# First batch element of a delta-rule and MLP-mixer kernel: block layout by vector transposes, zero products on TensorE, a new order of loads and steps

## The chip, the cores and the metric

The kernel runs on one core of one Trainium2 chip. Its engines are TensorE (PE; its weight loads are shown as PEld), VectorE (DVE), ScalarE (ACT), GpSimd (POOL) and SyncE (SP, which here issues nearly all DMAs). The metric is the device time of one execution in microseconds. The kernel before takes 851.35 us (median of three runs).

## The reference

Four batch elements, 8 heads of 48 numbers, 768 steps of time. For each head a 48x48 state is carried through time (the delta rule); its reads, with heads side by side (768x384), go through an MLP mixer: first over time (768 to 256 to 768), then over channels (384 to 1536 to 384).

```python
k_n = k / (np.linalg.norm(k, axis=-1, keepdims=True) + 1e-06)
for t in range(S):
    y[:, :, t] = np.einsum('bhd,bhde->bhe', q[:, :, t], state)
    v_old = np.einsum('bhde,bhd->bhe', state, kt)
    state = state + bt[:, :, :, None] * np.einsum('bhd,bhe->bhde', kt, vt - v_old)
...
h = np.maximum(xt @ w_tok1, 0.0) @ w_tok2          # xt: x with time last
u = x + h.transpose(0, 2, 1)
out = u + np.maximum(u @ w_ch1, 0.0) @ w_ch2
```

## The kernel before

**Units and steps.** The time of a batch element is cut into 6 units of 128 steps (`u` counts them through: 0 to 5 are the first element's), a unit into two chunks of 64. Inside a chunk the recurrence is solved in closed form: a triangular 64x64 matrix per head has to be inverted. Between chunks the state is carried.

**What is done for a unit.** `load_kq` loads keys and queries (`kpad`, `qpad`, and the keys a second time as `kst`). `prep` computes norms, turns keys and queries (`p_t`, L308 and L325), writes the turned keys to the block-diagonal `kbd` (one buffer), multiplies (`p_g`, L338) and masks the products into `gm` (DVE, L340). The triangular blocks' 32x32 diagonal parts are then inverted for several units at once, a *round* (`invert`): 30 steps of two DVE instructions each (L373, L377), with one block per partition. To get the blocks there, four DMAs per unit write them from `gm` to DRAM (L356) and one DMA reads them with a block in each partition (L367); afterwards one DMA writes the inverses (L384), and `fetch_w` reads them into `wt`, four DMAs per unit (L395). `join` makes the 64x64 inverses from the 32x32 ones (DVE transposes `t`, L407; products `p_z`, `p_x`).

**The recurrence.** `recur` is one chunk: `p_q` (PE), `r_bd` (DVE), `p_w` (PE), `w_bd` (ACT), `p_s` (PE), the new state `s_bd` (DVE, L486). The next chunk's `p_q` needs that state. In the first batch element each part is cut into two halves of the heads. The first element has 12 such chunks, called steps 0 to 11 here.

**The mixer.** `mixer(b)` needs all 12 chunks of element b: `p_1` (L510), `p_h` (L523), whose sum into `xb` is a DVE addition (L527), then for 6 groups of 128 time steps a turn `p_ut`, `p_c` (L549) and `p_o` (L564). While the mixer of one element runs, the units of the next are computed between its matmuls.

**Weights.** `round_weights` rounds the float64 weights to float32 in pieces: a load into `d` (L177), two ACT and two DVE instructions, an addition on POOL (L193), one more DVE instruction (L195). There are 6 pieces of 256 columns for `w1`, 4 of 384 for `w2`, 12 for `wc1` and 12 for `wc2`.

**Order.** Every function is a generator; `at(time, dt, fn, ...)` sets a time of its own scale (one unit of the first element is 1) for its first part and the distance of the next ones, and `run_plan` issues the parts in order of these times. Each engine executes its instructions in an order fixed when the program is built. Rounds are units [0, 1], [2, 3, 4, 5], then four each.

Of the kernel before, what the change touches and what calls it, by code (L numbers as in the profile page):

```python
# [23 lines left out]
def kernel(  # L24
# [70 lines left out]

    ident = const.tile([128, 128], FP32, name="ident")
# [9 lines left out]

    nc.scalar.sqrt(const.tile([1, 1], FP32, name="warm"), ident[0:1, 0:1])

# [4 lines left out]
    NW = 3  # L113
    NK = 3
# [22 lines left out]
    for t in gms:  # L137
        pad = t[:, 0 : NB * GW].rearrange("s (b three n) -> s b three n", b=NB, n=DP)
        nc.vector.memset(pad[:, :, 1, D:DP], 0.0)
        nc.gpsimd.memset(t[:, NB * GW :], 0.0)  # L140
    for t in t11s + wts + [zst]:
        nc.gpsimd.memset(t, 0.0)
# [9 lines left out]

    def load_beta():

        rows = mlp_pool.tile([B * H, S], FP32, name="b_rows", tag="xb")
        nc.scalar.dma_start(out=rows, in_=beta.rearrange("b h s -> (b h) s"))
# [8 lines left out]
        nc.scalar.copy(beta_st.rearrange("s b p c -> s c (b p)"), p_b)  # L165
        yield

    def round_weights(dst, src):
# [23 lines left out]
        )  # L192
        nc.gpsimd.tensor_tensor(out=f, in0=f, in1=lo, op=ALU.add)  # L193
# [25 lines left out]
    xins = {}  # L219
    xouts = {}  # L220
    rounds = [[0, 1], [2, 3, 4, 5]]
# [4 lines left out]
    turning = set()  # L226
    walked = set()
# [8 lines left out]
    def load_kq(u):  # L236
        b, c = divmod(u, NCH)
        ksts[u] = kst = loads.tile([128, NP, 2, D], FP32, name="kst")
# [16 lines left out]
    def load_v(u):  # L255
        vsts[u] = v_st = loads.tile([128, NP, 2, D], FP32, name="v_st")
        stacked(v_st, v, u)
        yield
        nc.gpsimd.tensor_tensor(
            out=v_st, in0=v_st,  # L260
            in1=nrms[u % NV][:, :, :, None].to_broadcast([128, NP, 2, D]), op=ALU.mult,
        )

# [6 lines left out]
    def gm_of(u):  # L270
        return gms[u % NV][:, 0 : NB * GW].rearrange(
            "s (b three n) -> s b three n", three=3, n=DP
        )

    def wt_of(u):
        return wts[u % NW][:, 0 : NB * C].rearrange("s (b n) -> s b n", n=C)

    def prep(u):
# [12 lines left out]
        )  # L291
        nrm_f = nrm.rearrange("s p c -> s (p c)")
# [3 lines left out]
        rec = work.tile([128, NB], FP32, name="rec")  # L296
        nc.vector.reciprocal(rec, nrm_f)
# [19 lines left out]
        nc.gpsimd.tensor_tensor(  # L317
# [5 lines left out]
        p_t = ps_prep([128, NP, 2, C], "p_t")  # L323
# [3 lines left out]
        nc.gpsimd.tensor_tensor(  # L327
# [3 lines left out]
        if u + NK < NU:  # L331
            load_kq(u + NK)
# [19 lines left out]
        for par in range(2):  # L352
            for i in range(2):
                lo = (4 * j + 2 * par + i) * NB
                row = C * par + HB * i
# [309 lines left out]
```

## Time and profile before

| | us |
|---|---|
| runs, median (lowest to highest) | 851.35 (850.71 to 854.84) |
| profiled execution | 852.24 |
| its span, first to last instruction | 850.4 |
| PE busy | 732.3 |
| DVE busy | 394.8 |
| ACT busy | 253.0 |
| POOL busy | 111.6 |

The span is 1.84 us shorter than the execution that it was taken from. Busy shares over the span mean little here: the first 202 us, in which the first batch element's units are computed, and the rest, in which mixers fill PE, have different limits. Mean granted TensorE clock over the span is 0.924 of full speed. "Released by" or an arrow `<-` in a row names what ended the idle time before an instruction.

### The profile page before, as it was taken

What the parts mean: (1) busy time and instruction counts of PE and PEld (TensorE: products, weight loads), DVE (VectorE), ACT (ScalarE), POOL (GpSimd) and SP (SyncE); (2) the same over time, 40 slices, a digit from 0 to 9 for tenths busy, and PEclk for the clock granted to TensorE, in tenths of its full rate; (3) what the DMA queues carried; (4) which work ended last, traced back from release to release, by engine and by line L of the source; (5) the groups of instructions that cost most, each with busy time, mean ns of one, the idle gap of its engine ahead of it and who ended that gap; (6) DMA issues with size and microseconds to landing.
All of it is one profiled execution on the core that took longest, in us unless ns stands there. A gap on an engine that the chain in (4) does not pass through costs nothing.

```text
span 850.4 us, 13384 instructions
## 1 busy us (share of the span) xinstructions
PE 732.3 (86%) x5080; PEld 606.6 (71%) x5080; DVE 394.8 (46%) x1081; ACT 253.0 (30%) x596; POOL 111.6 (13%) x142
## 2 busy tenths in 40 slices
PE   5630654969689999999999899999999999999998
PEld 4620644856469797887787888886898888678876
DVE  4487775756973459333267323493229422010000
ACT  5430422744234522333231333311332222111110
POOL 4322112223430211002000001110000000000000
PEclk9765755987899999999999999999999999999999
DMA  7763414445433441224122223202110200000000
GB/s 137 138 144 63 107 28 126 71 82 155 121 109 53 71 94 24 68 44 78 29 48 54 43 49 69 46 19 53 22 39 20 44 11 10 9 1 20 11 9 19
DMA packets 164591, 49.73 MB, mean 58 GB/s; under 512 B 155536, under 2 KB 158608, under 8 KB 164528
## 3 DMA queue, kind: packets, MB, share of 16 engines
q1 hardware_dynamic: 164480, 48.79, 26.6%
q8 instruction: 40, 0.66, 0.3%
q14 instruction: 23, 0.19, 0.1%
q10 hardware_dynamic: 48, 0.10, 0.0%
HBM read 37.85 MB, written 11.01 MB: 57 GB/s over the span
## 4 chain that ended last, share of the span: by engine, by line
PE 49%; DVE 9%; DMA 2%; ACT 2%; issue 1%; SPq 1%; ACTq 0%
PE p_c L549 16%; PE p_o L564 15%; DVE x L377 3%; DVE sub L373 3%; PE p_h L523 3%; PE p_s L482 2%; PE p_g L338 2%; PE p_q L453 2%; PE p L510 2%; PE p_w L470 2%; PE p_x L422 1%; PE p_z L413 1%; SPq L251 1%; PE p_ut L533 1%; DMA kst<-in_k_dram 1%
## 5 line engine op out<-in xcount | busy, mean ns | idle before, releaser
L549 PE MATMUL p_c<-u_t,wc 128*128 128x128 f32 x1728 | 218.2, 280 | 2.5 <-ACT u_t L537 1.8
L549 PEld LDWEIGHTS p_c<-u_t,wc 128*128 128x128 f32 x1728 | 206.5, 195 | 7.8 <-ACT u_t L537 2.5
L564 PE MATMUL p_o<-wc,r 128*128 128x384 f32 x576 | 197.5, 490 | 3.1 <-DVE wc L195 3.1
L564 PEld LDWEIGHTS p_o<-wc,r 128*128 128x128 f32 x576 | 105.0, 191 | 64.8 <-DVE wc L195 4.4
L556 ACT ACTIVATE r<-p_c 128x512 f32<-128x512 f32 x72 | 43.0, 597 | 156.8 <-PE p_c L549 156.4
L373 DVE TENSOR_TENSOR sub<-x 128x84 f32<-128x84 f32 (+22 forms) x210 | 77.3, 368 | 22.9 <-DMA x<-n_dram 18.3
L377 DVE TENSOR_TENSOR x<-x,sub 128x84 f32<-128x84 f32 (+22 forms) x210 | 76.7, 365 | 4.7
L338 PE MATMUL p_g<-kqt,kbd 128*128 128x128 f32 x384 | 60.1, 313 | 17.9 <-ACT kqt L326 17.7
L413 PE MATMUL p_z<-t,gm 128*65 128x64 f32 x384 | 30.7, 236 | 50.2 <-DVE t L407 49.8
L338 PEld LDWEIGHTS p_g<-kqt,kbd 128*128 128x128 f32 x384 | 55.1, 223 | 24.0 <-ACT kqt L326 22.5
L570 DVE TENSOR_TENSOR xb<-xb,p_o 128x384 f32<-128x384 f32 x24 | 13.3, 554 | 116.2 <-PE p_o L564 116.0
L413 PEld LDWEIGHTS p_z<-t,gm 128*65 128x65 f32 x384 | 28.7, 151 | 52.7 <-issue 28.5
L486 DVE TENSOR_TENSOR s_bd<-s_bd,p_s 64x192 f32<-64x192 f32 (+1 forms) x100 | 31.6, 316 | 73.9 <-PE p_s L482 72.2
L482 PE MATMUL p_s<-w_bd,gm 128*128 128x96 f32 x384 | 58.5, 297 | 5.2 <-ACT w_bd L474 4.9
L482 PEld LDWEIGHTS p_s<-w_bd,gm 128*128 128x128 f32 x384 | 52.6, 208 | 10.3 <-ACT w_bd L474 9.1
L340 DVE TENSOR_TENSOR gm<-p_g,mb 128x512 f32<-128x512 f32 x48 | 33.0, 690 | 57.3 <-PE p_g L338 55.0
L453 PE MATMUL p_q<-s_bd,kqt 128*128 128x96 f32 x352 | 50.9, 287 | 4.2 <-DVE s_bd L486 3.9
L453 PEld LDWEIGHTS p_q<-s_bd,kqt 128*128 128x128 f32 x352 | 47.1, 201 | 9.6 <-issue 3.0
L470 PE MATMUL p_w<-r_bd,wt 128*65 128x96 f32 x384 | 45.5, 263 | 7.2 <-issue 3.5
L455 DVE TENSOR_TENSOR r_bd<-v_st,p_q 64x192 f32<-64x192 f32 (+1 forms) x110 | 34.8, 316 | 35.1 <-PE p_q L453 23.0
L459 ACT ACTIVATE xb<-p_q 64x384 f32<-64x384 f32 (+1 forms) x55 | 23.0, 419 | 92.7 <-DVE r_bd L455 92.4
L474 ACT COPY w_bd<-p_w 64x192 f32<-64x192 f32 (+1 forms) x120 | 33.5, 280 | 54.0 <-PE p_w L470 52.0
(70 smaller groups left out, 708.8 us busy)
## 6 DMA issues: line engine op xcount, KB each, us to landing
d<-in_moe_w_ch_dram SPq DMA_DIRECT2D x24, 384.0 KB, 3.3
kpad<-in_k_dram SPq DMA_DIRECT2D x24, 192.0 KB, 3.5
kst<-in_k_dram SPq DMA_DIRECT2D x96, 48.0 KB, 2.6
qpad<-in_q_dram SPq DMA_DIRECT2D x24, 192.0 KB, 3.6
v_st<-in_v_dram SPq DMA_DIRECT2D x96, 48.0 KB, 2.6
out_dram<-xb SPq DMA_DIRECT2D x24, 192.0 KB, 1.9
n_dram<-gm SPq DMA_DIRECT2D x96, 32.0 KB, 1.7
wt<-w_dram SPq DMA_DIRECT2D x96, 32.0 KB, 2.1
```

The lines of the kernel that those rows point to most:

```text
L338: nc.tensor.matmul(p_g[:, i], kbd[:, nb], kqt[:, nb])
L373: nc.vector.tensor_tensor(out=tmp, in0=x[:, 0:s, s : s + 1].to_broadcast([n, s, w]), in1=x[:, s : s + 1, s + 1 : HB].to_broadcast([n, s, w ...
L377: nc.vector.tensor_tensor(out=x[:, 0:s, s + 1 : HB], in0=x[:, 0:s, s + 1 : HB], in1=tmp, op=ALU.add,)
L413: nc.tensor.matmul(p_z[0:65, nb], gm[:, lo : lo + 65], t11[:, nb])
L453: nc.tensor.matmul(p_q[:, p], kqt[:, 2 * p + cc], s0[:, p])
L455: nc.vector.tensor_tensor(out=r_bd[r, hp, e], in0=v_st[r, hp, cc], in1=p_q[hi, hp, e], op=ALU.subtract,)
L470: nc.tensor.matmul(p_w[0 : C + 1, p], wts[u % NW][:, w_lo : w_lo + C + 1], r_bd[:, p])
L474: nc.scalar.copy(w_bd[r, hp, e], p_w[lo, hp, e])
L482: nc.tensor.matmul(p_s[:, p], gm[:, 2 * p + cc, 0:2], w_bd[:, p])
L549: nc.tensor.matmul(p_c[:, i], wc1[:, cb, f * 128 : (f + 1) * 128], u_t[:, cb], start=(cb == 0), stop=(cb == NCB - 1),)
L556: nc.scalar.activation(r, p_c, ACTF.Relu)
L564: nc.tensor.matmul(p_o, r2[f // FG][:, f % FG], wc2[:, f], start=(f == 0), stop=(f == NHT - 1),)
```

## The change

In rounds of the first batch element (units 0 to 5) the blocks no longer go through DRAM: `to_parts` copies each of a unit's four sets of 8 blocks to a tile `turned` (two copies on DVE, two on ACT), one DVE transpose of 128x1024 puts each block into a partition, and after the inversion one more brings it back; `from_parts` copies it into `gm`, where `join` and `recur` now read it (`wt` is gone in all elements; the other elements keep the DRAM path). The rounds are [0, 1, 2, 3], [4, 5], then as before. `keep_warm` issues products of a zero tile by zeros: 7 and 19 of 512 columns at two places before the recurrence, and three of 256 columns in each step of the first element. For units 0 to 3 two scalings (`mb` and the keys' part of `gm`) move from POOL to DVE. `kpad`, `qpad` and `kst` have four buffers (they had three, three and two), the first element's `p_t` takes another set of PSUM buffers, and beta's load moves to SP. The square in `round_weights` is written in place (no `w_a`). The first element's plan is a table of times; the others' nearly keep theirs.

```diff
+    warm = const.tile([128, 129], FP32, name="warm")
+    nc.vector.memset(warm, 0.0)
+    nc.scalar.sqrt(warm[0:1, 128:129], warm[0:1, 128:129])
...
-    nc.scalar.sqrt(const.tile([1, 1], FP32, name="warm"), ident[0:1, 0:1])
...
+    def keep_warm(n, m=4):
+        p = ps_prep([128, m, 128], "p_warm")
+        zero = warm[:, 0:128]
+        for _ in range(n):
+            nc.tensor.matmul(p, zero, zero[:, None, :].to_broadcast([128, m, 128]))
...
-    rounds = [[0, 1], [2, 3, 4, 5]]
+    rounds = [[0, 1, 2, 3], [4, 5]]
...
-        ksts[u] = kst = loads.tile([128, NP, 2, D], FP32, name="kst")
+        ksts[u] = kst = loads.tile([128, NP, 2, D], FP32, name="kst", bufs=NK)
...
-        p_t = ps_prep([128, NP, 2, C], "p_t")
+        ps_turn = ps_mlp if u < NCH else ps_prep
+        p_t = ps_turn([128, NP, 2, C], "p_t")
...
-        nc.gpsimd.tensor_tensor(
+        scaler = nc.vector if u in EARLY_SC else nc.gpsimd
+        scaler.tensor_tensor(
             out=mb, in0=mask_c[:, None, None, :].to_broadcast([128, NP, 2, C]),
...
+    def to_parts(u):
+        rnd, j = round_of[u]
+        if u < NCH:
+            t = turned_of(rnd)
+            for i, (block, at_t, _) in enumerate(quarters(u)):
+                on = nc.vector.tensor_copy if i in EARLY_DVE else nc.scalar.copy
+                on(out=t[at_t].rearrange("s t b -> s b t"), in_=block)
+            return
...
+    def from_parts(u):
+        rnd, j = round_of[u]
+        assert rnd in turned_back
+        if u < NCH:
+            for i, (block, at_t, _) in enumerate(quarters(u)):
+                on = nc.vector.tensor_copy if i in EARLY_DVE else nc.scalar.copy
+                on(out=block, in_=xins[rnd][at_t].rearrange("s t b -> s b t"))
...
-        x = work.tile([RU * 4 * NB, HB, HB], FP32, name="x", bufs=1)[0:n]
-        nc.sync.dma_start(out=x, in_=xins.pop(rnd)[0:n])
+        x = work.tile([128, HB, HB], FP32, name="x", bufs=1)[0:n]
+        if early:
+            nc.vector.transpose(x.rearrange("b s t -> b t s"), xins[rnd])
+        else:
+            nc.sync.dma_start(out=x, in_=xins.pop(rnd)[0:n])
...
+        if early:
+            nc.vector.transpose(xins[rnd], x.rearrange("b s t -> b t s"))
...
+        if b == 0 and WARM_R:
+            keep_warm(1, WARM_R)
         yield
...
+    INVERT = {0: (-2.4, 0.0594), 1: (0.1, 0.0422)}
+    WARM = [(-98.95, 7), (-2.3, 19)]
+    WARM_R = 2
+    EARLY_SC = (0, 1, 2, 3)
+    EARLY_DVE = (1, 3)
...
-    at(6.0, 0.05, load_weights, (wc2, moe_w_ch2))
+    at(*WEIGHTS[2], load_weights, (wc2, moe_w_ch2))
```

On PE, from the last unit that is prepared before the recurrence to the first chunk, before stood this (`kqt` with its number is a unit's turned keys and queries, 105 the sixth's):

```order
L308 MATMUL p_t<-ident,kpad_89 128x128 x4
L325 MATMUL p_t<-ident,qpad_92 128x128 x4
L338 MATMUL p_g<-kqt_105,kbd 128x128 x8
L413 MATMUL p_z<-t_0_115,gm_94 65x64 x8
L422 MATMUL p_x<-wt_112,zst 65x32 x8
L470 MATMUL p_w<-r_bd,wt_112 65x96 x4
L482 MATMUL p_s<-w_bd,gm_94 128x96 x4
```

and now stands this (101 is the fourth unit, 102 and 103 the fifth and sixth):

```order
L367 MATMUL p_g<-kqt_101,kbd 128x128 x8
L156 MATMUL p_warm<-warm 128x512 x19
L356 MATMUL p_t<-ident,qpad_92 128x128 x4
L338 MATMUL p_t<-ident,kpad_89 128x128 x4
L356 MATMUL p_t<-ident,qpad_93 128x128 x2
L367 MATMUL p_g<-kqt_102,kbd 128x128 x8
L356 MATMUL p_t<-ident,qpad_93 128x128 x2
L367 MATMUL p_g<-kqt_103,kbd 128x128 x8
L487 MATMUL p_z<-t_110,gm 65x64 x8
L496 MATMUL p_x<-gm,zst 65x32 x8
L156 MATMUL p_warm<-warm 128x256 x2
L548 MATMUL p_w<-r_bd,gm 65x96 x4
```

The fifth and sixth units' products come behind 19 products of zeros, and from the first chunk on zeros stand between the chunk's own products.

On DVE, from the last step of the first round to the first transposes of `join`, before stood:

```order
L373 TENSOR_TENSOR sub<-x 64x30
L377 TENSOR_TENSOR x<-x,sub 64x30
L195 SCALAR_TENSOR_TENSOR w_153<-w_a,w_f 128x384
L294 TENSOR_SCALAR nrm_106<-nrm_106 128x8
L297 RECIPROCAL rec<-nrm_106 128x8
L298 TENSOR_TENSOR rec<-rec 128x8
L299 TENSOR_TENSOR cs<-rec,beta_st 128x8
L407 STREAM_TRANSPOSE t_0_115<-wt_112 32x8x32 x2
```

and now stands:

```order
L458 TENSOR_TENSOR sub<-x 128x30
L462 TENSOR_TENSOR x<-x,sub 128x30
L469 STREAM_TRANSPOSE turned<-x 128x1024
L316 TENSOR_REDUCE ksum<-ksq 128x8
L434 COPY gm<-turned 32x8x32 x2
L482 STREAM_TRANSPOSE t_110<-gm 32x8x32 x2
L450 STREAM_TRANSPOSE x<-xb 128x32x32
```

Between the last step and `join` stand a transpose, a sum and two copies where a DMA to DRAM and four from it were, and the second round's blocks come in right behind.

On DVE in the first mixer, where the first two of the six additions of `p_h` stand among the third round's steps and weight pieces, before:

```order
L373 TENSOR_TENSOR sub<-x 128x220
L527 TENSOR_TENSOR xb<-xb,p_h 128x384
L377 TENSOR_TENSOR x<-x,sub 128x11x20
L185 TENSOR_SCALAR w_f<-d_1844 128x384
L373 TENSOR_TENSOR sub<-x 128x228
L189 SCALAR_TENSOR_TENSOR w_f<-d_1844,w_f 128x384
L377 TENSOR_TENSOR x<-x,sub 128x12x19
L527 TENSOR_TENSOR xb<-xb,p_h 128x384
```

and now, with three of them:

```order
L462 TENSOR_TENSOR x<-x,sub 128x5x26
L610 TENSOR_TENSOR xb<-xb,p_h 128x384
L458 TENSOR_TENSOR sub<-x 128x150
L610 TENSOR_TENSOR xb<-xb,p_h 128x384
L462 TENSOR_TENSOR x<-x,sub 128x6x25
L610 TENSOR_TENSOR xb<-xb,p_h 128x384
L458 TENSOR_TENSOR sub<-x 128x168
```

One instruction stands between two additions where there were five.

## Rows read from the trace of the kernel before

**Rows 1.** Busy by stretch: PE, PEld, DVE, ACT, POOL; then clock, DMA share, GB/s.

```profile
0.00:48.37 48.37, 29.15 (x176) 25.70 (x176) 22.30 (x66) 23.42 (x50) 19.90 (x42) 0.82 0.74 140
48.37:78.67 30.30, 3.71 (x16) 3.48 (x16) 28.95 (x83) 5.60 (x12) 6.06 (x7) 0.58 0.47 96
78.67:93.25 14.58, 6.58 (x46) 6.13 (x46) 6.42 (x21) 2.79 (x10) 3.86 (x7) 0.50 0.64 167
93.25:131.40 38.15, 18.76 (x116) 16.02 (x115) 31.81 (x104) 12.84 (x37) 7.41 (x7) 0.63 0.21 45
131.40:148.13 16.73, 8.02 (x62) 7.84 (x62) 7.53 (x21) 5.01 (x15) 3.17 (x3) 0.50 0.47 118
148.13:202.24 54.11, 43.21 (x348) 39.27 (x348) 34.26 (x105) 29.26 (x83) 12.05 (x13) 0.85 0.47 96
202.24:253.00 50.76, 38.74 (x154) 25.28 (x154) 44.81 (x120) 17.51 (x37) 20.86 (x20) 0.90 0.40 120
253.00:851.00 598.00, 584.11 (x4169) 482.92 (x4167) 218.76 (x566) 156.53 (x353) 38.27 (x45) 1.00 0.18 38
```

**Rows 2.** Whom PE waited for, 78 to 202 us: total, times, longest.

```profile
PE p_z L413 <- DVE t L407: 46.6, 2, 28.1
PE p_x L422 <- DMA wt<-w_dram: 6.2, 1, 6.2
```

**Rows 3.** Timeline: start, length, and in brackets the idle time before; units 0 and 3.

```profile
12.73 3.42 PE L338 MATMUL p_g<-kqt,kbd 128*128 128x128 f32 x16 [1.01 <-ACT kqt L326]
...
32.33 3.46 PE L338 MATMUL p_g<-kqt,kbd 128*128 128x128 f32 x16 [1.38 <-ACT kqt L326]
```

**Rows 4.** Groups, whole span: busy us, mean ns of one.

```profile
L340 DVE TENSOR_TENSOR gm<-p_g,mb 128x512 f32<-128x512 f32 x48 | 33.0, 690 | 57.3 <-PE p_g L338 55.0 <-POOL gm L327 2.0
...
L407 DVE STREAM_TRANSPOSE t<-wt 32x256 f32<-32x256 f32 x48 | 20.8, 433 | 43.1 <-DMA wt<-w_dram 41.3 <-PE p_z L413 1.1
```

**Rows 5.** Groups of DVE, 48.37 to 78.67 us: the round's steps, weight pieces.

```profile
L377 DVE TENSOR_TENSOR x<-x,sub 64x30 f32<-64x30 f32 (+14 forms) x30 | 12.1, 402 | 0.7
L373 DVE TENSOR_TENSOR sub<-x 64x30 f32<-64x30 f32 (+14 forms) x30 | 10.9, 364 | 0.7
L195 DVE SCALAR_TENSOR_TENSOR w<-w_a,w_f 128x384 f32<-128x384 f32 (+1 forms) x5 | 3.2, 644 | 1.0 <-POOL w_f L193 1.0
L189 DVE SCALAR_TENSOR_TENSOR w_f<-d,w_f 128x384 uint32<-128x384 uint32 x4 | 2.2, 543 | 0.0
...
L185 DVE TENSOR_SCALAR w_f<-d 128x384 uint32<-128x384 uint32 x4 | 1.4, 346 | 0.0
```

**Rows 6.** Timeline: second transpose of the first `join`, first new state.

```profile
84.33 0.43 DVE L407 STREAM_TRANSPOSE t<-wt 32x256 f32<-32x256 f32 x1 [0.39 <-DMA wt<-w_dram]
...
93.25 0.26 DVE L491 COPY s_bd<-p_s 64x96 f32<-64x96 f32 x1 [1.33 <-PE p_s L482]
```

**Rows 7.** Timeline: the new state of step 5; the first mixer's start.

```profile
154.14 1.08 DVE L486 TENSOR_TENSOR s_bd<-s_bd,p_s 64x96 f32<-64x96 f32 x4 [1.54 <-PE p_s L482]
...
202.24 8.50 PE L510 MATMUL p<-xb,w 128*128 128x384 f32 x24
```

**Rows 8.** Chain that ended last, by time: PE at full clock in the last mixer.

```profile
766.78 8.04 PE p_c L549 x72
775.15 7.74 PE p_o L564 x24
```

**Rows 9.** Timeline: a DVE instruction beside one of POOL, and its like alone.

```profile
17.30 1.04 POOL L317 TENSOR_TENSOR mb<-mask_c,cs 128x512 f32<-128x512 f32 x1 [4.28 <-DVE cs L299]
17.40 1.23 DVE L189 SCALAR_TENSOR_TENSOR w_f<-d,w_f 128x256 uint32<-128x256 uint32 x1
...
22.35 0.41 DVE L189 SCALAR_TENSOR_TENSOR w_f<-d,w_f 128x256 uint32<-128x256 uint32 x1
```

**Rows 10.** Timeline of the first mixer: first wait for an addition, first `p_c`.

```profile
217.81 1.56 PE L523 MATMUL p_h<-r,w 128*128 128x384 f32 x4 [1.82 <-DVE xb L527]
...
228.28 5.49 PE L549 MATMUL p_c<-u_t,wc 128*128 128x128 f32 x24 [1.22 <-ACT u_t L537]
```

More of the change, by code (lines that the diff above doesn't have):

```diff
@@ L136 @@
     nc.vector.memset(kbd, 0.0)
[L137 to L141, printed above, removed]
+    nc.vector.memset(gmb[:, :, DP + D : 2 * DP], 0.0)
+    nc.gpsimd.memset(gm_all[:, NV * NB * GW :], 0.0)
+    for t in [t11, zst]:
         nc.gpsimd.memset(t, 0.0)
@@ L226 @@
     turning = set()
+    masked = set()
+    inverted = set()
+    joined = set()
+    scaled = set()
+    turned_back = set()
+    beta_in = []
+    steps = []
     walked = set()
@@ L262, in load_v @@
         )
+        scaled.add(u)
     def blocks(t):
@@ L348, in prep, with turned_of @@
         turning.remove(u)
-        rnd, j = round_of[u]
+        to_parts(u)
+        masked.add(u)
+        if 8 <= u + NK < NU:
+            load_kq(u + NK)
+        yield
+    xins = {}
+    xouts = {}
+    def turned_of(rnd):
+        if rnd not in xins:
+            if rnd == 0:
+                xins[rnd] = const.tile([128, HB, RU * NB], FP32, name="turned")
+            else:
+                xins[rnd] = mlp_pool.tile([128, HB, RU * NB], FP32, name="xb", tag="xb")
+            if len(rounds[rnd]) < RU:
+                nc.gpsimd.memset(xins[rnd][:, :, len(rounds[rnd]) * NB :], 0.0)
+        return xins[rnd]
@@ L350, in prep @@
         if j == 0:
             xins[rnd] = dram.tile([RU * 4 * NB, HB, HB], FP32, name="n_dram")
[L352 to L355, printed above, removed]
+        for block, _, rows in quarters(u):
+            nc.sync.dma_start(out=xins[rnd][rows].rearrange("b s t -> s b t"), in_=block)
+    def from_parts(u):
[5 more added lines that the diff above has]
+                on(out=block, in_=xins[rnd][at_t].rearrange("s t b -> s b t"))
+        else:
+            for block, _, rows in quarters(u):
@@ L356, in prep @@
                 nc.sync.dma_start(
-                    out=xins[rnd][lo : lo + NB].rearrange("b s t -> s b t"),
-                    in_=gm[row : row + HB, :, 2, HB * i : HB * i + HB],
+                    out=block, in_=xouts[rnd][rows].rearrange("b s t -> s b t")
                 )
-        yield
+        inverted.add(u)
     def invert(rnd):
-        n = 4 * NB * len(rounds[rnd])
-        x = work.tile([RU * 4 * NB, HB, HB], FP32, name="x", bufs=1)[0:n]
-        nc.sync.dma_start(out=x, in_=xins.pop(rnd)[0:n])
+        early = rounds[rnd][0] < NCH
@@ L429, in join @@
             )
+        joined.add(u)
         yield
@@ L435, in recur @@
         u, cc = divmod(t, 2)
+        assert t == len(steps) and u in joined and u in scaled
+        steps.append(t)
         gm, kqt, v_st = gm_of(u), kqts[u % NV], vsts[u]
```

206 lines of the change are left out of this document (138 added, 68 removed).

## Prediction, made before the change was timed

> **What bounds the kernel now.** I read first the busy time by stretch [rows 1], with borders at the events of the first batch element. From 253 us on PE is busy 584 of 598 us at full clock: that part is PE's own work, and the change leaves it there. All that can be won lies before. Stretch by stretch, the reader is to see: while units 0 to 5 are prepared (0 to 48.37) no engine is full. In the first round (48.37 to 78.67) DVE is, 28.95 of 30.30. Then come 14.58 us until the first new state, with all engines below half. From 93.25 to 131.40 steps 0 to 3 share DVE with the second round: DVE 31.81 of 38.15. From 131.40 to 148.13 the blocks of that round are on their way and step 4 waits. Steps 4 to 11 take the 54.11 us to 202.24, and the first mixer's opening (to 253) has DVE at 44.81 of 50.76 and PE at 38.74. The waits of PE say the same [rows 2]: of 78 to 202 us it stood 46.6 us, in two waits, for the transposes of `join`, which wait for the two rounds and their blocks, and 6.2 us for one unit's blocks from DRAM. The clock is low there: 0.50 to 0.63 in four of the stretches, 0.85 in steps 4 to 11 [rows 1].
>
> So there are three things: DVE's work in the rounds, the way of the blocks, and which units a round holds. I follow them up to the first mixer's start, 202.24 us before [rows 7].
>
> **The change part by part.**
>
> *Preparing four units instead of six ahead of the first round.* Before, the product of unit 0 begins at 12.73 us and that of unit 3 at 32.33, so one unit costs 6.5 us [rows 3]. With four `kst` buffers the loads run ahead, a second PSUM set lets a unit's transposes go ahead of the last one's product, and `kbd`, still one buffer, makes the loop. DVE now has the two scalings and two copies more per unit. The first unit waits for beta behind six other DMAs of SP, which I put at 1 us. Bounds: at 6.5 us a unit, 12.7 + 19.6 + 3.5 for the product + 2 for mask and copies = 38; at 5 us a unit, 34. I take 34.5, since the first unit's waits on ACT's tables go too. The first round thus starts 13.9 us earlier than at 48.37.
>
> *The first round, now with four units.* Its 30 steps are as many, 23.0 us by the sums of 60 instructions [rows 5]: a step's length hangs on the columns, and blocks lie in partitions. Added by the order within the round: ten weight pieces where the old round had four and a half (3.2 + 2.2 + 1.4 = 6.8 us, so 1.5 us each of 384 columns [rows 5]; six of the ten have 256 columns, so 12 to 15 us, I take 13.5): +6.7. Two masks more at 0.69 [rows 4]: +1.4. Four copies: no row has them, they have the size of the small transposes at 0.433 [rows 4]: +1.7. Two transposes of 1024 elements a partition, also without a row: between one and four times 0.433, I take 1.25 each, nearer the upper end since they have four times the elements: +2.5. Together +12.3, so 42.6 us, from 34.5 to 77.1. What was gained in front is used up: the round ends 1.6 us earlier, but it holds units 0 to 3.
>
> The 19 products of zeros stand on PE ahead of units 4 and 5 within this round. By columns, a product of 128 columns takes 8.04 / 36 = 0.22 us at full clock and one of 384 columns 7.74 / 12 = 0.65 (two rows of the trace are one product) [rows 8], so 512 columns 0.86 and 19 of them 16 us, at half clock 33. DVE reaches unit 4's masks some 22 us into its round: at full clock the zeros end at 34.5 + 16 = 51, well before; at half clock 11 us later than DVE wants them. I take no cost.
>
> *The way back.* Before, from the round's end (78.67) to the first new state (93.25) 14.58 us. Now: transpose 1.25, two copies 0.87 (the other two beside them on ACT), one small transpose 0.43, and from the second one on as before, 93.25 - 84.33 = 8.9 [rows 6], where PE is cold as then. 11.5 us: the first new state at 88.6.
>
> *Steps 0 to 4 beside the second round (units 4 and 5).* Nothing shortens DVE's share: before, 38.15 us with DVE at 83% held four steps and most of a round, 104 instructions [rows 1]. By order 105 stand there now: one step more, two weight pieces less, and one of them a big transpose (1.25). I take 39.7, and 2.5 more for the products up to the new state of step 5: 130.8. Before it stood at 154.14 [rows 7]. This is where the change earns: the wait for the second round's blocks (16.73 us) falls on steps that no longer need them, since units 2 and 3 are there.
>
> *Steps 5 to 11.* Before, from 154.14 to 202.24, 48.1 us. The 6.2 us for blocks from DRAM [rows 2] go: 41.9. Against that, DVE has by order 117 instructions between these two points where it had 82 (more weight pieces, and the copies), at a mean of 34.26 / 105 = 0.33 us [rows 1] 38 us where it was 27; and 14 products of zeros of 256 columns (0.43 each, 6 us) stand between the products. PE was busy 43.21 of 54.11 there [rows 1], so not all of this fits beside. I take 4 us: 46. Bounds: 42 (all hidden) and 54 (half of DVE's 11 and all zeros show). The first mixer then starts at 176.8, 25.4 us earlier.
>
> At this place a rule bears on the sum. The row: a DVE instruction that takes 0.41 us alone took 1.23 when a POOL instruction of 1.04 us had begun just before it [rows 9]. The Trainium skill (SBUF — State Buffer, Who interferes with whom) says that a DVE instruction with two SBUF inputs and a POOL instruction that reads SBUF exclude each other, and the later one waits for the whole of the first. That row agrees. By the rule every POOL instruction among a round's steps is paid by DVE. Without it the sum above stands, because means from the old stretches hold such waits already; with it the extra POOL work is a result of its own, the second rival.
>
> *The first mixer's opening.* Before, PE stood 50.76 - 38.74 = 12.0 us [rows 1], from the first wait for an addition at 217.81 on, and `p_c` began at 228.28 cold: 24 rows in 5.49 us [rows 10], where the same at full clock is 24 / 72 of 8.04 = 2.7 [rows 8]. The additions now stand one instruction apart, so `p_h` should run through, `p_c` begin some 19 us after the start instead of 26, and PE stay warm. The last weight pieces come as late as before: DVE has by order 127 instructions up to the last one, 122 before, which at the old pace makes 50.76 x 127 / 122 = 53 us. PE's work that needs no later piece (`p_1`, `p_h`, two groups) is four times 7.74 and two times 8.04 [rows 8], 47 us, where `p_1` and `p_h` have 24 rows of 384 columns as `p_o` has, so 4 to 5 us of waiting remain. I take 8 us; bounds 0 (the pieces hold PE anyway) and 12.
>
> *No effect expected.* Memsets, the in-place square (a piece's buffer is held longer, with three of them and some 3.3 us between pieces), the fewer DMAs on SP, and the later elements, whose path is the old one but for `wt`: all lie beside a busy PE.
>
> **The sum.** -25.4 - 8 = -33.4 from the profiled execution's 852.24: 818.8. The runs' median is 0.9 us lower, which is below what I can tell. Forecast 819, own range 806 to 832.
>
> **The rivals.**
>
> 1. *The steps run faster.* If zeros keep PE at full clock, a step lasts about what it did from 148.13 to 154.14 [rows 1, 7] and less. For it: at half clock the step's own three products take twice as long. Against: DVE is 83% busy in steps 0 to 3, and no clock of PE helps that. Taking 5.2 us for steps 5 to 11 and 35 us for steps 0 to 4: 10 + 5 us less, 804.
>
> 2. *DVE and POOL exclude each other throughout.* In the old round POOL had 7 instructions in 6.06 us [rows 1]; the order has about 20 in the new one, 17 us. If each microsecond more costs DVE 0.8 (0.82 of 1.04 [rows 9]), the round is 9 us longer, and half as much more is lost in steps 0 to 11 and the mixer: +13, 832; with the big transposes at their upper end and pieces that arrive late 840.
>
> 3. *The gain is given back later.* The first mixer starts early, but the last weight pieces and the third round on DVE end when they did relative to it, and the second element's units come late: PE waits there. For it: PE waited 14 us after 253 too [rows 1]. Against: all follow the same plan. Price: the mixer's 8 and 6 more, 833.
>
> 4. *Slower: the zeros don't hold the clock, and PE becomes the bound of the steps.* From 78.67 to 202.24 PE was busy 6.58, 18.76, 8.02 and 43.21 us at clocks of 0.50, 0.63, 0.50 and 0.85 [rows 1], which is 56 us at full clock; 36 products of zeros add 15.5. At half clock these 71 us last 142, so the mixer starts at 77 + 142 = 219 and the time is 852.2 + 17 - 8 = 861. It decides from a mean clock of about 0.54 on (71 / 0.54 = 132, a start at 210). For it: clocks of 0.50 to 0.63 in these stretches. Against: in steps 4 to 11, where PE was busy 80% of the time, the clock was 0.85, and with the zeros at half clock PE would be without a gap. If the change in this way doesn't do what it says but DVE still sets the pace, nothing is lost and the forecast stands.
>
> **How the numbers follow.** Forecast 0.52 (806 to 832), first rival 0.14, second 0.16, third 0.09, fourth 0.09 with all of its lesser forms (0.03 of it within 0.5%, 0.06 slower). A change of 0.5%, 4.3 us, is about what a measurement of this kernel can tell from none. Faster by more: 0.91; within: 0.03; slower: 0.06. The range has to reach into the first two rivals and leaves out the fourth: 801 to 839.
>
> **What would show it.** In the profile after: the first round's big transpose at 33 to 38 us and its end at 75 to 81, DVE over 90% busy between; the first new state about 11 us after that; no wait of PE for `join` longer than the first one; the state of step 5 at 127 to 136; `p_1` at 168 to 186; `p_c` 18 to 21 us after it and at full clock; and from there to the end about as much as the old 598 us and what the opening leaves. It would be wrong if the first round ended after 90 us, if the clock stayed at half through the steps, or if the time from `p_1` to the end grew.

## The result, and the profile after

The changed kernel takes 822.59 us (median of four runs, 822.04 to 822.88), the kernel before in the same session 852.79 us. The ratio is 0.9645, with a 95% interval of 0.9616 to 0.9674. The profiled execution has a span of 820.8 us at a mean clock of 0.969 (before: 850.4 us).

Busy time by stretch, with borders at the first round's begin and end, the first new state and the first mixer's start as in [rows 1], at step 5's state in place of the two borders there between these, and at the opening's end (50.76 us as before). Columns as there.

```profile
0.00:39.46 39.46, 29.63 (x169) 22.20 (x170) 21.11 (x56) 20.67 (x40) 4.44 (x18) 0.87 0.64 120
39.46:84.04 44.58, 21.07 (x76) 12.53 (x75) 42.85 (x109) 15.39 (x33) 16.78 (x20) 0.77 0.50 107
84.04:99.00 14.96, 8.32 (x52) 7.14 (x53) 13.04 (x32) 9.50 (x22) 1.35 (x1) 0.54 0.24 85
99.00:134.49 35.49, 32.34 (x276) 27.98 (x275) 33.11 (x107) 17.41 (x53) 2.67 (x3) 1.00 0.17 35
134.49:180.58 46.09, 40.69 (x318) 35.10 (x316) 36.64 (x118) 27.26 (x80) 16.53 (x17) 0.96 0.53 114
180.58:231.34 50.76, 43.09 (x222) 31.50 (x221) 44.70 (x116) 21.77 (x45) 21.01 (x20) 0.97 0.48 136
231.34:820.80 589.46, 578.27 (x4101) 475.24 (x4099) 220.36 (x579) 154.86 (x351) 40.60 (x47) 1.00 0.18 38
```

The first state comes later than before (99.00, was 93.25), but step 5's comes 19.7 us earlier: steps 1 to 5 take 35.49 us (before 60.89, from 93.25 to 154.14), in which DVE and PE are both over 90% busy, at full clock. The stretch of 16.73 us in which step 4 waited for the second round's blocks is gone. The mixer starts 21.7 us earlier, and from there to the end 640.2 us pass, 7.9 less than before.

PE's waits from 78 to 181 us (total, times, longest), against [rows 2]: one long wait for `join` is left where there were two, 46.6 us together.

```profile
PE p_z L487 <- DVE t L482: 21.0, 1, 21.0
PE p_x L496 <- issue: 2.4, 1, 2.4
```

Timelines of the same run, first the products of units 0, 1 and 3, against [rows 3]: unit 0's at full clock, the others' at half (granted 0.54 to 0.55 in the products of units 1 to 3).

```profile
14.11 2.05 PE L367 MATMUL p_g<-kqt,kbd 128*128 128x128 f32 x16 [1.50 <-ACT kqt L357]
19.40 3.67 PE L367 MATMUL p_g<-kqt,kbd 128*128 128x128 f32 x16 [2.36 <-ACT kqt L357]
...
33.32 3.54 PE L367 MATMUL p_g<-kqt,kbd 128*128 128x128 f32 x16 [2.46 <-ACT kqt L357]
```

DVE's groups in the first round, 39.46 to 84.04 us (busy us, mean ns), against [rows 5]:

```profile
L462 DVE TENSOR_TENSOR x<-x,sub 128x30 f32<-128x30 f32 (+14 forms) x30 | 13.4, 445 | 0.2
L458 DVE TENSOR_TENSOR sub<-x 128x30 f32<-128x30 f32 (+14 forms) x30 | 12.2, 405 | 0.4
L199 DVE SCALAR_TENSOR_TENSOR w_f<-d,w_f 128x256 uint32<-128x256 uint32 (+1 forms) x10 | 5.3, 532 | 0.0
L207 DVE SCALAR_TENSOR_TENSOR w<-d,w_f 128x256 f32<-128x256 f32 (+1 forms) x10 | 5.3, 531 | 0.9 <-POOL w_f L205 0.9
L195 DVE TENSOR_SCALAR w_f<-d 128x256 uint32<-128x256 uint32 (+1 forms) x10 | 4.3, 429 | 0.0
...
L450 DVE STREAM_TRANSPOSE x<-turned 128x1024 f32<-128x1024 f32 x1 | 2.0, 1990 | 0.6 <-ACT turned L421 0.6
```

The steps cost 25.6 us where they cost 23.0. Why they cost more shows in the timeline of DVE and POOL in that round: a step that starts behind a POOL instruction ends with it, 1.02 us, where the next larger one takes 0.27. Nine of the 60 steps take 0.76 to 1.12 us in this way, the rest at most 0.60.

```profile
42.32 1.04 POOL L348 TENSOR_TENSOR mb<-mask_c,cs 128x512 f32<-128x512 f32 x1 [37.20 <-DVE cs L328]
42.45 1.02 DVE L458 TENSOR_TENSOR sub<-x 128x84 f32<-128x84 f32 x1
...
44.29 0.27 DVE L458 TENSOR_TENSOR sub<-x 128x108 f32<-128x108 f32 x1
```

The way back, from the transpose to the first state, against [rows 6]:

```profile
84.04 1.91 DVE L469 STREAM_TRANSPOSE turned<-x 128x1024 f32<-128x1024 f32 x1
85.98 5.11 ACT L434 COPY gm<-turned 32x256 f32<-32x256 f32 x8 [5.16 <-DVE turned L469]
87.20 0.90 DVE L482 STREAM_TRANSPOSE t<-gm 32x256 f32<-32x256 f32 x2
...
91.76 0.75 ACT L491 COPY zst<-p_z 32x256 f32<-32x256 f32 x2
...
94.37 2.48 PE L156 MATMUL p_warm<-warm 128*128 128x256 f32 x4
96.64 1.45 PE L548 MATMUL p_w<-r_bd,gm 128*65 128x96 f32 x8
...
99.00 1.10 DVE L571 COPY s_bd<-p_s 64x96 f32<-64x96 f32 x4 [1.35 <-PE p_s L562]
```

ACT copies the blocks of all four units before it gets to `zst` of the first `join`, and PE, near half clock (0.54 in this stretch), runs zeros ahead of `p_w`.

Step 5's state, the mixer's start and its first `p_c` stand in the timeline so, against [rows 7, 10]: `p_c` comes 19.0 us after the start, and its 72 rows take 9.93 us, 1.9 us more than at full clock [rows 8].

```profile
134.49 0.53 DVE L566 TENSOR_TENSOR s_bd<-s_bd,p_s 64x96 f32<-64x96 f32 x2
...
180.58 7.93 PE L593 MATMUL p<-xb,w 128*128 128x384 f32 x24
...
199.55 9.93 PE L632 MATMUL p_c<-u_t,wc 128*128 128x128 f32 x72 [2.17 <-ACT u_t L620]
```

### The profile page after: what moved, and what is told of

Read it like the earlier page. It is cut to its first block, busy times and chain, and to the rows that moved or that the text cites. A ratio compares the mean times of both kernels' runs of the same rounds, so it can differ in the third digit from the quotient of the medians.

```text
span 820.8 us, 13554 instructions
## 1 busy us (share of the span) xinstructions
PE 753.4 (92%) x5204; PEld 611.7 (75%) x5204; DVE 411.8 (50%) x1115; ACT 266.9 (33%) x619; POOL 103.4 (13%) x126
## 4 chain that ended last, share of the span: by engine, by line
PE 61%; DVE 22%; ACT 6%; DMA 4%; issue 4%; SPq 3%; POOL 1%; ACTq 0%; POOLq 0%; DVEq 0%
PE p_o L648 17%; PE p_c L632 16%; DVE sub L458 6%; PE p_g L367 5%; DVE x L462 5%; PE p_s L562 4%; PE p_q L530 3%; PE p_h L606 3%; PE p L593 3%; PE p_w L548 3%; PE p_z L487 2%; PE p_x L496 2%; ACT kbd L345 2%; SPq L272 2%; DMA kst<-in_k_dram 1%
## 5 line engine op out<-in xcount | busy, mean ns | idle before, releaser
L632 PE MATMUL p_c<-u_t,wc 128*128 128x128 f32 x1728 | 215.1, 278 | 2.7 <-ACT u_t L620 2.7
L458 DVE TENSOR_TENSOR sub<-x 128x30 f32<-128x30 f32 (+22 forms) x210 | 77.4, 369 | 12.7 <-DMA x<-n_dram 8.2
L462 DVE TENSOR_TENSOR x<-x,sub 128x30 f32<-128x30 f32 (+22 forms) x210 | 76.3, 363 | 4.0
L562 PE MATMUL p_s<-w_bd,gm 128*128 128x96 f32 x384 | 54.4, 279 | 2.9 <-ACT w_bd L552 2.3
L562 PEld LDWEIGHTS p_s<-w_bd,gm 128*128 128x128 f32 x384 | 48.4, 191 | 8.6 <-ACT w_bd L552 7.5
L530 PEld LDWEIGHTS p_q<-s_bd,kqt 128*128 128x128 f32 x352 | 45.2, 191 | 8.2 <-issue 2.2
L530 PE MATMUL p_q<-s_bd,kqt 128*128 128x96 f32 x352 | 48.3, 275 | 2.4 <-DVE s_bd L566 2.3
L156 PE MATMUL p_warm<-warm 128*128 128x256 f32 (+1 forms) x124 | 47.9, 511 | 1.5 <-DVE warm L98 1.1
L487 PE MATMUL p_z<-t,gm 128*65 128x64 f32 x384 | 28.5, 227 | 22.0 <-DVE t L482 21.9
L205 POOL TENSOR_TENSOR w_f<-w_f,d 128x384 uint32<-128x384 uint32 (+1 forms) x34 | 37.1, 1092 | 79.1 <-DVE w_f L199 35.6
```

Of the source, the lines that this page charges most:

```text
L156: nc.tensor.matmul(p, zero, zero[:, None, :].to_broadcast([128, m, 128]))
L458: nc.vector.tensor_tensor(out=tmp, in0=x[:, 0:s, s : s + 1].to_broadcast([n, s, w]), in1=x[:, s : s + 1, s + 1 : HB].to_broadcast([n, s, w ...
L462: nc.vector.tensor_tensor(out=x[:, 0:s, s + 1 : HB], in0=x[:, 0:s, s + 1 : HB], in1=tmp, op=ALU.add,)
L487: nc.tensor.matmul(p_z[0 : C + 1, nb], weights_of(u, nb), t11[:, nb])
L530: nc.tensor.matmul(p_q[:, p], kqt[:, 2 * p + cc], s0[:, p])
L562: nc.tensor.matmul(p_s[:, p], gm[:, 2 * p + cc, 0:2], w_bd[:, p])
```

## The experiments

All kernels compute everything. Marks of each profiled run, in us: first new state, start of the first mixer (`p_1`), last of the 34 weight pieces on DVE, span.

| | runs, median | first state | `p_1` | last piece | span |
|---|---|---|---|---|---|
| before | 851 to 853 | 93.25 | 202.24 | 250.9 | 850.4 |
| after | 822.59 | 99.00 | 180.58 | 235.6 | 820.8 |
| no zeros | 832.86 | 98.17 | 181.75 | 242.6 | 831.1 |
| no step zeros | 831.58 | 96.95 | 181.72 | 242.5 | 829.5 |
| path through DRAM | 842.62 | 101.67 | 190.19 | 254.3 | 839.4 |
| before, new rounds | 857.28 | 110.31 | 206.46 | 253.0 | 856.6 |
| old rounds | 841.88 | 87.48 | 201.39 | 242.8 | 843.2 |
| weights early | 825.58 | 94.26 | 176.98 | 232.3 | 819.4 |
| copies on POOL | 820.65 | 98.08 | 178.48 | 234.0 | 820.3 |
| zeros in preparation | 823.52 | 94.26 | 178.06 | 233.8 | 820.4 |
| half zeros | 832.05 | 95.72 | 181.87 | 243.3 | 829.1 |
| pieces into steps | 844.33 | 94.67 | 187.52 | 228.7 | 842.4 |
| all of these | 825.92 | 96.84 | 185.58 | 225.9 | 824.9 |
| zeros in steps 0 to 5 | 826.85 | 96.48 | 175.20 | 237.1 | 821.9 |

**The blocks' path and the rounds.** One part of the change taken out at a time. First the path (`from_parts` is edited in the same way):

```diff
     def to_parts(u):
         rnd, j = round_of[u]
-        if u < NCH:
-            t = turned_of(rnd)
...
     def invert(rnd):
-        early = rounds[rnd][0] < NCH
+        early = False
```

> The changed kernel, but the blocks of the first element's two rounds go through DRAM as before (four DMAs to, one from, one to, four from for each unit or round), with rounds, zeros and order as changed. DVE loses 24 copies and four transposes of 1024 elements a partition, about 24 x 0.4 + 4 x 1.95 = 17 us. Theory A (DVE's work sets the pace, and the waits for blocks went by the choice of rounds): the first round starts 3 to 5 us later and the first new state comes 3 to 5 us after the round's end later, and DVE gives back up to 10: 818 to 828. Theory B (the path through DRAM was the loss): two round trips of 6 to 9 us each on the path, 834 to 842.

Measured: 842.62 us (836.63 to 845.52), ratio to before 0.989 (0.983 to 0.995): 0.6 us beyond the upper end of theory B. Its reason shows only in part. The first round's steps and the way back in this run, then what held up the round, and a wait of DVE in the mixer's opening:

```profile
50.56:84.35 33.79, 4.08 (x21) 3.55 (x19) 32.83 (x94) 9.46 (x21) 11.27 (x15) 0.60 0.51 116
84.35:101.67 17.32, 9.19 (x52) 7.88 (x52) 8.94 (x25) 4.22 (x12) 2.98 (x3) 0.50 0.65 135
...
29.29 16.57 PE L156 MATMUL p_warm<-warm 128*128 128x512 f32 x38
...
46.34 0.59 ACT L342 COPY kqt<-p_t 128x512 f32<-128x512 f32 x1 [7.40 <-PE p_t L338]
...
49.07 0.55 DVE L316 TENSOR_REDUCE ksum<-ksq 128x8 f32<-128x384 f32 x1 [9.29 <-ACT ksq L314]
...
199.66 0.56 DVE L600 TENSOR_TENSOR xb<-xb,p_h 128x384 f32<-128x384 f32 x1 [5.66 <-PE p_h L596]
```

The steps begin at 50.56 us, in the changed kernel at 41.49, and end at 84.35, there at 84.01. The path is not alone to blame for the late begin: the load of the blocks is issued at 40.22 and lands 4.6 us later, but DVE stands until 49.07 at `ksum` of a later unit, which waits for ACT, and ACT waits for keys that PE turns behind the 19 products of zeros. On the way back DVE idles 8.4 us (there 1.9).

The span is 18.6 us longer than the changed kernel's, in three parts: 2.7 us at the first state, 6.9 from there to `p_1`, and 9.0 behind `p_1`. In the last part no block of this element is on its way any more; DVE waits 5.66 us at the first addition of `p_h`, as in the kernels without zeros below, and the last weight piece comes 64.1 us behind `p_1` instead of 55.0. So this run puts at most 9.6 us down to the path itself.

From the first round's begin (39.46, and 40.00 in this run) to `p_1` the direct path gives DVE 12 us more to do (125.6, with DRAM 113.2), but it idles 15.5 us where it idled 37.0.

Then the new rounds in the kernel before:

```diff
-    rounds = [[0, 1], [2, 3, 4, 5]]
+    rounds = [[0, 1, 2, 3], [4, 5]]
-                at(-3.5 + 0.3 * j, 0.06, prep, u)
+                at(-4.1 + 0.3 * j, 0.06, prep, u)
```

> The kernel before with the rounds [0, 1, 2, 3], [4, 5] and the first four units' preparation 0.6 earlier in the order so that the first round finds them; path through DRAM, no zeros, no other edit. Theory A (the choice of rounds removes the wait of 16.7 us ahead of step 4): 8 to 14 us faster than the kernel before, a ratio of 0.984 to 0.991. Theory B (the rounds gain only with the direct path and the zeros): within 3 us of the kernel before, or slower, since the first round waits for two more units and the clock stays at half in the steps.

Measured: 857.28 us, ratio 1.0077 (1.0048 to 1.0106), so 0.8% slower. The first round's begin and the first state in this run's timeline, and PE's waits for `join`:

```profile
58.24 0.18 DVE L373 TENSOR_TENSOR sub<-x 128x30 f32<-128x30 f32 x1
...
110.31 0.26 DVE L491 COPY s_bd<-p_s 64x96 f32<-64x96 f32 x1 [4.57 <-PE p_s L482]
...
PE p_z L413 <- DVE t L407: 58.2, 3, 51.0
```

Two units more are prepared and inverted first: the round begins 9.9 us later and the first state comes 17.1 us later, about as much as the stretch ahead of step 4 was long. One wait of 51.0 us stands where the longest was 28.1. Theory A fails: the choice of rounds alone moves the wait to the front.

And the old rounds in the changed kernel, with units 2 to 5 prepared during the first round:

```diff
-    rounds = [[0, 1, 2, 3], [4, 5]]
+    rounds = [[0, 1], [2, 3, 4, 5]]
...
-        2: (-72, 0.5),
-        3: (-68, 0.5),
+        2: (-2.25, 0.08),
+        3: (-1.7, 0.08),
...
```

> The changed kernel with the old rounds [0, 1], [2, 3, 4, 5]; direct layout and zeros stay, units 2 to 5 are prepared while the first round runs. Theory A (with the direct path the choice of rounds pays, since step 4 needs no second round): the first round starts near 26 us and the first new state comes near 85, but step 4 waits for a second round whose steps stand among steps 0 to 3; its state comes at 130 to 138 where it came at 128, and the time is 825 to 833 us. Theory B (the direct path is all of the gain): 819 to 824. If old rounds are better with it: below 819.

Measured: 841.88 us, ratio 0.9876 (0.9841 to 0.9911): further than theory A said, on its side. The wait of PE for the second round is back:

```profile
PE p_z L487 <- DVE t L482: 39.6, 2, 21.5
```

So without either of the two parts the time is 842 us, 19 to 20 us more than with both. With the old rounds the loss lies ahead of `p_1` (20.8 us); with the path through DRAM half of it lies behind. That both kernels stay 10 us below the kernel before can't be put down to the part that each keeps, since both also hold the zeros and the new plan.

**The zeros.** One kernel without any, and one with the second of these edits alone, in which the 26 ahead of the recurrence stay:

```diff
-    WARM = [(-98.95, 7), (-2.3, 19)]
+    WARM = []
-    WARM_R = 2
+    WARM_R = 0
```

> The changed kernel without any product of zeros (neither the 7 and 19 ahead of the recurrence nor the three of each step). Theory A, DVE sets the pace of the rounds and of steps 0 to 5 (33.1 of 35.5 us busy there), so the clock earns little: 824 to 828 us, and the way from the first new state to step 5's stays under 38 us. Theory B, the full clock that the zeros bring is what made these steps shorter than the old four: PE's 32.3 us less 8 of zeros are 24 at full clock and 48 at half, so the stretch takes about 48 us where it takes 35.5, and the time is 835 us or more. Theory C, the zeros only stand in the way: 816 to 820.

> The changed kernel without the three products of zeros in each step; the 26 ahead of the recurrence stay. Theory A (DVE sets the pace): 821 to 825. Theory B (the steps are short by the clock that their own zeros hold): about what all zeros together are worth, 833 or more, with a granted clock below 0.8 between the first new state and step 5. If the real products of units 4 and 5 and of the steps hold the clock by themselves: 819 to 822, since up to 15 us of PE's work go.

Measured: 832.86 and 831.58 us, ratios 0.979 (0.976 to 0.982) and 0.977 (0.972 to 0.981). In number that is nearer to theory B of both, but for its reason only in part. Steps 1 to 5, and the stretch from there to the mixer's start, without step zeros:

```profile
96.95:138.05 41.10, 30.20 (x210) 26.39 (x209) 32.38 (x106) 15.80 (x51) 2.73 (x4) 0.71 0.14 28
138.05:181.72 43.67, 34.84 (x300) 30.42 (x300) 37.42 (x120) 28.09 (x79) 15.44 (x16) 1.00 0.54 114
```

The clock falls to 0.71 and steps 1 to 5 take 5.6 us longer; but steps 6 to 11, without zeros in PE's row, take 2.4 us less, the first state is 2.1 us earlier, and the mixer starts only 1.1 us later. The other 7.6 us are lost behind that, where DVE and ACT wait:

```profile
DVE xb L610 <- PE p_h L606: 5.5, 1, 5.5
...
189.05 0.49 ACT L601 ACTIVATE r<-p 128x384 f32<-128x384 f32 x1 [6.47 <-PE p L593]
```

The changed kernel has no such wait on DVE, and ACT waits 2.4 us. Its order puts the first addition of `p_h` 30 DVE instructions behind the last one of the last state; without step zeros it stands 16 behind, DVE gets there before PE has the product, and the weight pieces queued behind it wait too. On ACT the next piece stands behind `r`, which waits for the products of `p_1`. Two more kernels try to part clock and order: zeros of half the size, and zeros in steps 0 to 5 alone.

```diff
-    WARM_R = 2
+    WARM_R = 1
```

> The changed kernel with step zeros of 128 columns each in place of 256; the 26 ahead of the recurrence stay. Theory A (the zeros work through the clock: without them steps 0 to 5 ran at 0.71 to 0.74 and took 40 us): if half of them hold the clock too, PE has 4 us less to do in a stretch where it was busy 32.3 of 35.5 us, and the time is 820 to 823; if they do not, the clock falls below 0.9 there and the time is 826 to 832. Theory B (without zeros the order of DVE's instructions came out worse, and the clock has no part in it): 826 or more at a clock near 1.0 in the steps.

Measured: 832.05 us, ratio 0.979 (0.976 to 0.982). The clock is 0.89 from the first state to step 5's (38.3 us) and 0.89 from there to the mixer's start, so below 0.9, as theory A wanted for this time, but `p_1` comes only 1.3 us later than in the changed kernel. 7.0 us more pass behind it, and there the first addition, 19 behind, is not what DVE waits for:

```profile
189.19 0.49 ACT L601 ACTIVATE r<-p 128x384 f32<-128x384 f32 x1 [6.90 <-PE p L593]
...
191.95 0.56 DVE L207 SCALAR_TENSOR_TENSOR wc<-d,w_f 128x384 f32<-128x384 f32 x1 [7.00 <-POOL w_f L205]
```

The weight piece ahead of the addition waits for POOL, POOL for ACT's part of that piece, and ACT stands at `r`. So the place of the one addition isn't the whole cause: the pieces are held up on ACT too.

```diff
-        if b == 0 and WARM_R:
+        if b == 0 and c < 6:
```

> The changed kernel with step zeros in steps 0 to 5 alone; steps 6 to 11 have none. Without any step zeros the kernel lost 9 us, but its mixer started only 1.1 us later; in the mixer's opening DVE then stood 5.5 us at the first addition of p_h, which stood 19 instructions behind the last state's (31 in the changed kernel), and the last weight piece came 7 us later. Theory A (the clock of steps 0 to 5 is what the zeros earn): the clock there is 1.00 again, and the time is 822 to 824. Theory B (the zeros earn their 9 us by where the addition comes to stand in DVE's order, since here it stands 17 behind): steps 0 to 5 take 35 to 36 us and the mixer starts near 180.5 us as in the changed kernel, but DVE waits 4 to 6 us at the first addition, the last piece comes at 241 to 243, and the time is 828 to 831.

Measured: 826.85 us (823.72 to 827.51), ratio 0.971 (0.968 to 0.973), between the two; the profiled execution is the fastest of the five. Steps 1 to 5, the stretch up to the mixer's start, and DVE's wait:

```profile
96.48:130.84 34.36, 30.39 (x266) 26.52 (x265) 32.20 (x105) 15.79 (x49) 3.29 (x3) 1.00 0.17 36
130.84:175.20 44.36, 34.17 (x288) 29.21 (x289) 36.57 (x117) 27.20 (x78) 15.34 (x16) 1.00 0.53 111
```

```profile
DVE xb L610 <- PE p_h L606: 5.4, 1, 5.4
```

Full clock in steps 1 to 5 is worth 6.7 us there against the kernel without step zeros (34.36, 41.10), and 6.0 of it arrive at the mixer's start (78.7 us from the first state, 84.8 without). But the wait of theory B is there in its size (the addition stands 14 behind; the expectation, with 17, 19 and 31, counts from the begin of the state's row in the timeline), and from `p_1` to the end 646.7 us pass, 6.5 more than in the changed kernel. Both theories hold a part: by the medians 4.7 us are the zeros of steps 0 to 5 (the intervals of the two kernels just overlap), and 4.3 those of steps 6 to 11, where the clock is 1.00 without them; what changes there is the order. That the clock and not another effect of the early zeros makes the 4.7 is read from the clock column, not tried alone.

Nor does the good order belong to the zeros: the kernel with the path through DRAM has all of them and loses 9.0 us behind `p_1`. In the five kernels of this and the last part whose last piece comes 61 to 64 us behind `p_1`, 646.7 to 649.4 us pass from `p_1` to the end; in the changed kernel and the first three that follow the piece comes 55 to 56 us behind, and 640.2 to 642.4 pass. A kernel without zeros whose pieces keep the changed kernel's order was not tried.

**The terms that came out larger, and whether a gain there reaches the end.** Zeros behind a unit's products in `prep`:

```diff
+        if u < 3:
+            keep_warm(2)
         turning.remove(u)
```

> The changed kernel with two products of zeros (512 columns each) after the products of units 0, 1 and 2. Theory A (the preparation is a loop through p_g, kbd's copy and kqt, and p_g runs cold, 3.6 us where unit 0's took 2.05): p_g of units 1 to 3 takes 2.05 us, the first round starts 4 to 5 us earlier, at 35, and the time is 818 to 820. Theory B (the zeros stand ahead of the next unit's transposes and keep the gap): the round starts at 39 to 41, and the time is 822 to 825.

Measured: 823.52 us, ratio 0.967 (0.964 to 0.970). The last unit's product and the first transpose of the round:

```profile
29.32 2.05 PE L367 MATMUL p_g<-kqt,kbd 128*128 128x128 f32 x16 [0.59 <-ACT kqt L357]
...
33.98 2.00 DVE L452 STREAM_TRANSPOSE x<-turned 128x1024 f32<-128x1024 f32 x1 [0.36 <-ACT turned L423]
```

The mechanism of theory A holds (the round starts 5.5 us earlier), the end doesn't: 4.7 us earlier at the first state are 2.5 at `p_1`, 1.8 at the last piece and nothing in the runs. How much of the 5.5 the zeros earn is open: without them the same preparation began its round at 35.21 to 39.46 us in four kernels (last section).

```diff
                 on = nc.vector.tensor_copy if i in EARLY_DVE else nc.scalar.copy
+                if 0 < u < 4 and i not in EARLY_DVE:
+                    on = nc.gpsimd.tensor_copy
```

> The changed kernel with the copies of the inverses of units 1 to 3 on POOL where they are on ACT. In the changed kernel eight such copies hold ACT for 5.1 us after the first round, and the first join's copy waits behind them until 91.76 us. Theory A (that queue is the 3.5 us by which the way back was longer than forecast): the first new state comes near 96 instead of 99.0; since DVE sets the pace of the steps that follow, the end gains 1 to 3 us: 819.5 to 821.5. Theory B (POOL's copies hold up DVE's, as POOL's other work does, by about 0.8 us each): six of them cost 5 us, and the time is 823 to 828.

Measured: 820.65 us, ratio 0.963 (0.960 to 0.966): within theory A's range, but the first state moves by 0.9 us and not by 3. `zst` is copied 1.4 us earlier; the zeros ahead of `p_w` and the cold products stay. It is the lowest median, but its interval overlaps the changed kernel's.

```diff
-    WEIGHTS = [(-2.2, 0.25), (2.5, 0.3), (6.5, 0.05)]
+    WEIGHTS = [(-77, 1.2), (2.5, 0.3), (6.5, 0.05)]
```

> The changed kernel with the first ten weight pieces begun during the preparation of units 1 to 3 (start -77 at distances of 1.2 in place of -2.2 and 0.25). Theory A (the end hangs on DVE's work up to the last weight piece, at 235.6 us, 585 before the end; DVE idles 18 of the first 39.5 us): five pieces move ahead of the first round, 5 x 1.5 us, the round gets shorter by as much, and the last piece and the end come 5 to 8 us earlier: 815 to 818. Theory B (the preparation is a chain through DVE and ACT, in which each piece stands in the way, and DMAs are late): the round starts 4 us later or more, and the time is 820 to 826.

Measured: 825.58 us (821.14 to 827.62), ratio 0.968 (0.964 to 0.972). Five pieces go ahead of the round, which starts no later (39.37) and is 4.6 us shorter; `p_1` comes 3.6 and the last piece 3.3 us earlier in the profiled run, the fastest of four, whose span is 1.4 us shorter. The median shows no gain: theory A fails, and the late round of theory B is not seen either.

The last two kernels have the zeros in the preparation, the copies on POOL, and weight pieces moved into the steps; the second also has the early ones, as in the last edit, with (1.5, 0.25) and (4.6, 0.11) behind them.

```diff
-    WEIGHTS = [(-2.2, 0.25), (2.5, 0.3), (6.5, 0.05)]
+    WEIGHTS = [(-2.2, 0.25), (2.0, 0.22), (4.8, 0.1)]
```

> The changed kernel with zeros between the first units (first round at 34 us), POOL's copies for units 1 to 3, and the channel weights' pieces earlier (start 2.0 at 0.22 and 4.8 at 0.1 in place of 2.5 at 0.3 and 6.5 at 0.05). Theory A (the end hangs on the last weight piece, which the front's gain did not move by more than 2 us since the pieces' times are fixed against the steps; DVE idles 9.5 of 46 us in steps 5 to 11): four pieces move there, the last one comes near 226 us, and the time is 812 to 817. Theory B (the end hangs on the start of the mixer and what PE does from there, 640 us, and DVE's idle time in steps 5 to 11 is needed for their chain): the start comes at 178 to 182 and the time is 820 to 824.

> As the last one, with the first ten pieces begun in the preparation too (start -77 at 1.2) and the channel weights' from 1.5 at 0.25 and 4.6 at 0.11. Theory A: each part gives what it gave alone, 2 to 3 us at the mixer's start and 3 more at the last piece: 809 to 815. Theory B (the parts compete for the same idle time of DVE, and the end hangs on the mixer's start): 817 to 822.

Measured: 844.33 us, ratio 0.993 (0.990 to 0.995), and 825.92, ratio 0.970 (0.968 to 0.973). Both theories fail. In the first of them the last piece is early (228.7), but the pieces stand in front of the additions, all 34 of them ahead of the sixth, and PE waits for those:

```profile
PE p_h L610 <- DVE xb L614: 11.6, 2, 7.0
PE p_ut L620 <- DVE xb L614: 6.5, 1, 6.5
```

An early last piece alone is thus not what sets the end; here it was the additions that came late. In both kernels `p_1` also comes 5.0 to 6.9 us later than in the changed kernel: from the first state on DVE has 76.6 and 77.1 us of work there instead of 69.7.

## Why the prediction was right, step by step

The forecast was 818.8 from the profiled execution; that of the changed kernel is 822.65. The difference of 3.8 us is the sum of larger ones of both signs: the first state came 10.4 us later than forecast, and steps 1 to 5 gave back 6.7. That the total came out so near is in part luck.

- **Preparing four units**: forecast 34.5, measured 39.46, beyond its upper bound of 38. PE fell to half clock behind unit 0; with zeros there the products kept 2.05 us, a unit took 5.3, and the round started at 33.98. The forecast's 5 us a unit is nearly reached at full clock alone. With this, two signs were missed: the round's first transpose (33 to 38) and its end (75 to 81).
- **The first round**: forecast 42.6 with both large transposes, measured 46.5 (39.46 to 85.95). The transposes take 1.99 and 1.91 us, above the upper bound of 1.73; the steps 2.6 us more, the pieces 14.9 instead of 13.5. The steps' part is the second rival's mechanism: POOL had its 20 instructions (16.78 us), but the rival's 9 us for the round was too much, since only nine steps were held up in this way. The Trainium skill (SBUF — State Buffer, Who interferes with whom) states that the later of the two waits for the whole instruction of the first; the step of 1.02 us beside POOL's 1.04 agrees.
- **The way back**: the sum had the transpose back twice, 1.25 us to the good. Without it 10.25 were forecast and 13.05 measured: ACT's queue (`zst` 1.5 us late) and zeros ahead of `p_w`.
- **Steps 1 to 5**: forecast 42.2, measured 35.49. Here the first rival was right (35 us where the sum had 39.7 of the 42.2): the old stretch, whose pace the sum took over, ran at a clock of 0.63, and without step zeros, at 0.71, these steps take 41.10. DVE is 93% busy at full clock.
- **Steps 6 to 11**: forecast 46, measured 46.1; the first rival's other 10 us did not come.
- **Opening and rest**: forecast -8, measured 648.2 to 640.2; 6.5 us of it are waits of PE that went, 1.5 its shorter busy time. DVE's 127 instructions up to the last piece were named as the bound, with 53 us; they took 55.0. Beside 47 us of PE's work 53 leave 6 us of waiting, not the 4 to 5 of the sum; PE stood 7.7 us of the opening.
- **Third rival**: not in this change, but in three of the experiments: 2.1 to 3.6 us gained at the mixer's start are 0.4 to 1.4 of the span.
- **Fourth rival**: PE was 91% busy in steps 1 to 5, but at a clock of 1.00, not 0.54.

What the prediction had wrong is the credit. It put the gain down to the rounds, with the direct path as a means. The rounds alone cost 0.8%; the changed kernel with the old rounds, which keeps path, zeros and plan, has a third of the gain. The zeros stood in the sum with a price alone, and their gain only in the first rival; to take them out cost 9 to 10 us. Of that 7.6 to 9.1 came behind the mixer's start, from an order of the weight pieces that the sum did not price and that other edits spoil as well.

## What to carry to other kernels

A wait that a new grouping removes can come back at the front, as it did here when nothing else was changed: price the grouping, the path to the first group and the plan together. When a part is added to or taken out of a planned program, look at what that does to the order of engines that run strictly in sequence: in five of these kernels weight pieces queued behind a wait for the mixer's products, on DVE or on ACT, and the rest of the program took 6.5 to 9.1 us longer. Until the order is held the same, such a time is not the price of the part. A gain ahead of a stage that two engines must walk through in step counts only after that stage's end has been read.

## What was not expected of the hardware

- A DVE transpose of 128x1024 float32 takes 1.90 to 2.00 us, 4.5 times one of 256 elements a partition (0.43).
- The same preparation ran at different clocks in different executions: unit 3's product took 3.54 us in the changed kernel and, with the same instructions up to there, 2.05 in the kernel with half zeros, whose first round started at 35.21 instead of 39.46. The Trainium skill (TensorE: Matmul & The Clock Gate, Part 1: The HAM clock gate) says that the number of cold products differs between runs of one kernel; these rows agree.

```profile
30.55 2.05 PE L367 MATMUL p_g<-kqt,kbd 128*128 128x128 f32 x16 [1.62 <-ACT kqt L357]
```
